# Feed-forward weights and the last rows of wo in long rows per partition; the result stored from columns, without a transpose

## The chip, the cores and the metric

The kernel runs on one core of one Trainium2 chip. The core has five instruction streams: TensorE (PE, matmuls and their weight loads), VectorE (DVE), ScalarE (ACT), GpSimd (POOL) and SyncE (SP), which here only issues DMA transfers. The transfers run on 16 DMA engines that share the queue of SP. The metric is the device time of one launch in microseconds: 689.65 us before the change, the median of 3 runs (689.49 to 689.85).

## The reference

One token (a row of 640 features) goes through an attention block over a cache of 16384 keys and values for each of 32 heads, and then through a gated feed-forward block. Each block is preceded by a layer norm with shift and scale that come from a conditioning vector, and followed by a gate and a residual.

```python
mod = (_silu(c) @ w_mod).reshape(c.shape[0], 6, 1, -1)
sa, ca, ga, sb, cb, gb = (mod[:, i] ...)
h = _layernorm(x) * (1 + ca) + sa
q = (h @ wq)                       # 32 heads of 128
scores = q . k_cache * 128 ** -0.5 # 32 x 16384
o = softmax(scores) . v_cache      # 32 x 128
x = x + ga * (o @ wo)              # wo: 4096 x 640
h = _layernorm(x) * (1 + cb) + sb
x = x + gb * ((_silu(h @ w_gate) * (h @ w_up)) @ w_down)   # 640 x 1728, 1728 x 640
```

K and V are 4 MB each per head in bfloat16, 268 MB in all; all weights together are some 22 MB.

## The kernel before

**Columns.** A vector of 640 features is kept as a tile of 128 partitions by 5 columns (`KC` = 5). A product of a vector with a matrix is made on TensorE with the matrix as the stationary operand: for each piece of 128 output features and each piece of 128 input features there is one weight load of 128 x 128 and one matmul with a single moving column. So the result again stands in columns. Which features stand in which partition follows from how the matrix was loaded and which of its columns a matmul takes. For the first half of the program feature 5p+k stands in partition p, column k: `c_col`, `x_col`, `w_mod` and `wq` are loaded with `(p k)`, five neighbouring rows per partition, and `mod_mm_a` (line 321) takes every fifth column of `w_mod`, beginning at k. From `mod_mm_b` on (line 355: the gate, shift and scale vectors that are used after attention) the kernel changes to feature 128k+p: there, and in wo and w_down, a matmul takes 128 adjacent columns, and gate and up are loaded with `(k p)`, so that each partition receives five separate rows of 3456 bytes.

**Heads.** For each head, DVE multiplies K with the broadcast q, folds the product three times and reduces it to scores (lines 420 to 435). GpSimd takes maximum and sum over partitions, ACT the exponentials. PE then multiplies probabilities and V with V as the moving operand, 32 matmuls of 512 columns (line 459). For the last head V is loaded in three parts and is the stationary operand instead (line 483), so that its last part needs only 32 small matmuls.

**From heads to wo.** The heads 0 to 27 form the groups of `GROUPS`: three of 8 and one of 4. Wo's rows for a group of n heads are loaded so that a partition gets n neighbouring rows. The attention output of a head stands in order in the partitions, so it has to be rearranged to match: `on` scales it, `z` (line 496, ACT) spreads it over a mask into `Z`, one matmul `am` (line 500, PE) with a small selection matrix sums it into place, and `as` (line 502, ACT) copies the group to `A_sb`. The heads 28 to 31 (`HD` = 28) skip this: their part of wo is loaded one row of 1280 bytes per partition and head (`dma_wo_rows`), and `on` (line 505) writes them to `On`, from which wo's matmuls (line 541) take them directly.

**Feed-forward.** The rows of gate's output 256j+2p+i stand in partition p (`NP2` pairs), so that a partition gets pairs of rows of w_down, 2560 bytes; gate and up (line 605) therefore take every second column. A thirteenth piece of 128 features and a rest of 64 come in rows of 1280 bytes. W_down is loaded in five transfers and multiplied in five groups (line 623), each waiting for its own.

**Residual and result.** As the second half has feature 128k+p, x is loaded a second time as five rows (`x_row`), transposed on PE and copied to `x_res` in the middle of the loop over heads (line 550). At the end the 128 x 5 result `o_col` is transposed on PE (line 631), copied by ACT (line 632) and stored as five rows of 256 bytes.

**Order.** Each operation is given an engine, a position and the operations that it depends on; `_Plan.emit` sorts each engine's operations by position and puts a semaphore wait ahead of one whose dependency isn't yet known to be done. An engine works strictly in that order. The positions are written by hand: `TK(h)` is the start of head h, `TL` that of the last head, `TE` = `TL` + 32 the end part. SP issues K of the next head when the slot is free, then V; wo is issued in the next to last head (`TO`), gate, up and w_down behind the last scores (`TW`), as they lie in the slots of K.

Of the kernel before, what the change touches and what calls it, by code (L numbers as in the profile page):

```python
# [6 lines left out]
BF16 = mybir.dt.bfloat16  # L7
F32 = mybir.dt.float32
ALU = mybir.AluOpType
ACTF = mybir.ActivationFunctionType  # L10
# [26 lines left out]
class _Plan:  # L37
# [21 lines left out]
    def op(self, eng, pos, fn, deps=(), name=""):  # L59
        o = _Op(eng, pos, fn, list(deps), name, len(self.ops))  # L60
        self.ops.append(o)
        return o
# [79 lines left out]
def build(nc, A_x, A_k, A_v, A_wq, A_wo, B_wg, B_wu, B_wd, c_in, w_mod, out):  # L142
    H, S, Dh = A_k.shape[1], A_k.shape[2], A_k.shape[3]
    D = A_x.shape[2]
# [7 lines left out]
    NP2 = NF // 2  # L152
    GQ = 4

    GROUPS = [(0, 8), (8, 8), (16, 8), (24, 4)]
    HD = 28
    assert H % GQ == 0 and all(128 % n == 0 for _, n in GROUPS) and GROUPS[-1][0] + GROUPS[-1][1] == HD < H
# [5 lines left out]
    def TK(h):  # L163
        return 20.0 + PERIOD * h

    es = ExitStack()
    with es:
# [3 lines left out]
        def sb(name, shape, dtype):  # L171
            return es.enter_context(nc.sbuf_tensor(name, list(shape), dtype))
# [31 lines left out]
        A_sb = sb("A_sb", [128, HD], BF16)  # L204
        On = sb("On", [128, H - HD], BF16)
        x_row = sb("x_row", [KC, 128], BF16)
        o_row = sb("o_row", [KC, 128], BF16)
        x_res = sb("x_res", [128, KC], F32)
# [146 lines left out]
        o_mod_b = op(PE, 4.5, lambda e: f_mod(e, wm_v, 2, 6, lambda o, k: slice(o + 128 * k, o + 128 * (k + 1))), deps=[d_wm, o_h], name="mod_mm_b")  # L355
# [50 lines left out]
        for h in range(H):  # L406
# [82 lines left out]
            if h < HD:  # L489
                g = [i for i, (h0, n) in enumerate(GROUPS) if h0 <= h < h0 + n][0]  # L490
                h0, n = GROUPS[g]
                jw = 128 // n
                o_on[h] = op(ACT, base + 29.0, lambda e, h=h, sc=sc: e.activation(  # L493
                    out=on_f[:, h:h + 1], in_=OT_ps[:, h:h + 1], func=ACTF.Copy, scale=sc),
                    deps=[done, o_rl], name="on%d" % h)
                o_z[h] = op(ACT, base + 29.2, lambda e, h=h, g=g, n=n, o=(h - h0) * jw, jw=jw: e.activation(  # L496
                    out=Z[:, g, o:o + jw], in_=msk[n][:], func=ACTF.Copy, scale=on_f[:, h:h + 1]),
                    deps=[o_on[h], o_msk[n]], name="z%d" % h)
                if h == h0 + n - 1:
                    o_am = op(PE, base + 29.4, lambda e, g=g, n=n: e.matmul(A_ps[:, 0:n], lhsT=Z[:, g], rhs=e8[n][:], start=True, stop=True),  # L500
                              deps=[o_z[i] for i in range(h0, h0 + n)] + [o_e8[n], o_as[g - 1] if g else None], name="am%d" % g)
                    o_as[g] = op(ACT, base + 29.6, lambda e, h0=h0, n=n: e.activation(out=A_sb[:, h0:h0 + n], in_=A_ps[:, 0:n], func=ACTF.Copy),
                                 deps=[o_am], name="as%d" % g)
            else:
                o_on[h] = op(ACT, base + 29.0 + (0.7 if h == H - 1 else 0.0), lambda e, h=h, sc=sc: e.activation(
                    out=On[:, h - HD:h - HD + 1], in_=OT_ps[:, h:h + 1], func=ACTF.Copy, scale=sc),
                    deps=[done, o_rl], name="on%d" % h)
# [5 lines left out]
        while a < len(GROUPS):  # L513
            b = a
            while b < len(GROUPS) and GROUPS[b][1] == GROUPS[a][1]:
# [7 lines left out]
        d_wo1 = plan.dma(TO + 0.1, wo_v[:, HD:H, :], A_wo[HD * 128:H * 128, :].rearrange("(k p) n -> p k n", p=128),  # L523
                         "wo1", deps=[o_mod_b, o_mod], name="dma_wo_rows")
        wo_seq = [(k, g) for g, (h0, n) in enumerate(GROUPS) for k in range(h0, h0 + n)] + [(k, None) for k in range(HD, H)]
        o_wo = []
        for g in list(range(len(GROUPS))) + [None] * (H - HD):
            if g is not None:
                ks = [k for k, gg in wo_seq if gg == g]
                deps, pos = [o_as[g], d_wo[g]], TL + 29.45 + 0.005 * g  # L530
            else:
                k = HD + len(o_wo) - len(GROUPS)
                ks = [k]
                deps, pos = [o_on[k], d_wo1], TL + (29.48 + 0.001 * (k - HD) if k < H - 1 else 29.8)

            def f_wo(e, ks=ks):
                last = None
                for k in ks:
                    rhs = A_sb[:, k:k + 1] if k < HD else On[:, k - HD:k - HD + 1]
                    for cc in range(KC):  # L540
                        last = e.matmul(attn_ps[:, cc:cc + 1], lhsT=wo_v[:, k, 128 * cc:128 * (cc + 1)], rhs=rhs,
                                        start=(k == 0 and cc == 0), stop=(k == H - 1 and cc == KC - 1), skip_group_check=True)
                return last
            o_wo.append(op(PE, pos, f_wo, deps=deps, name="wo%d" % len(o_wo)))


        HX = H // 2
        d_xr = plan.dma(TK(HX) + 8.95, x_row[:], A_x[0, 0].rearrange("(k p) -> k p", p=128), "xr", name="dma_x_row")
        xT_bf = st_ps[:, 256:256 + KC].bitcast(BF16)
        o_xT = op(PE, TK(HX) + 29.9, lambda e: e.transpose(xT_bf[:, 0:KC], x_row[:], ident[0:KC, 0:KC]), deps=[d_xr, o_ident, o_rstd], name="x_tr")  # L550
        o_xf = op(ACT, TK(HX) + 29.95, lambda e: e.activation(out=x_res[:], in_=xT_bf[:, 0:KC], func=ACTF.Copy), deps=[o_xT], name="x_res")

# [3 lines left out]
        d_wg = plan.dma(TW, wg_v, B_wg.rearrange("(k p) n -> p k n", p=128), "wg", deps=wdeps, name="dma_wg")  # L556
        d_wu = plan.dma(TW + 0.01, wu_v, B_wu.rearrange("(k p) n -> p k n", p=128), "wu", deps=wdeps, name="dma_wu")
        wd_parts = []
        d_wd = []

        def load_wd(a, b):
            i = len(d_wd)
            if b <= 2 * NP2:
                dst = wd_v[:, a:b, :].rearrange("p (j i) n -> p j (i n)", i=2)
                src = B_wd[128 * a:128 * b, :].rearrange("(j p i) n -> p j (i n)", p=128, i=2)
            elif b <= NF:
                dst, src = wd_v[:, a, :], B_wd[128 * a:128 * b, :]
            else:
                dst, src = wd_v[0:FR, a, :], B_wd[128 * a:F, :]
            d_wd.append(plan.dma(TW + 0.02 + 0.01 * i, dst, src, ("wd", i), deps=wdeps, name="dma_wd%d" % i))  # L570
            wd_parts.append((a, b))
        for a, b in ((0, 6), (6, 2 * NP2 - 2), (2 * NP2 - 2, 2 * NP2)):
            load_wd(a, b)
        for a in range(2 * NP2, FCH):
            load_wd(a, a + 1)
# [7 lines left out]
            out=x1[:], in0=tt2[:], scalar=1.0, in1=x_res[:], op0=ALU.mult, op1=ALU.add, accum_out=st[:, 4:5]),  # L583
# [12 lines left out]
        def f_gu(e, wv, ps_t):  # L596
            last = None
            for j in range(FCH):
                for k in range(KC):
                    if j < 2 * NP2:  # L600
                        cols = slice(256 * (j // 2) + j % 2, 256 * (j // 2 + 1), 2)
                    else:
                        cols = slice(128 * j, min(128 * (j + 1), F))
                    w = 128 if j < NF else FR
                    last = e.matmul(ps_t[0:w, j:j + 1], lhsT=wv[:, k, cols], rhs=h2_col[:, k:k + 1],
                                    start=(k == 0), stop=(k == KC - 1))
            return last
# [9 lines left out]
        for i, (a, b) in enumerate(wd_parts):  # L617
            def f_down(e, a=a, b=b):
                last = None
                for cc in range(KC):  # L620
                    for k in range(a, b):
                        kw = 128 if k < NF else FR
                        last = e.matmul(f_ps[:, cc:cc + 1], lhsT=wd_v[0:kw, k, 128 * cc:128 * (cc + 1)], rhs=gu_col[0:kw, k:k + 1],  # L623
                                        start=(k == 0 and cc == 0), stop=(k == FCH - 1 and cc == KC - 1), skip_group_check=True)
                return last
            prev = op(PE, TE + 1.8 + 0.01 * i, f_down, deps=[o_gum, d_wd[i], prev], name="down%d" % i)
# [3 lines left out]
        oT_bf = A_ps[0:KC, 256:320].bitcast(BF16)  # L630
        o_tr = op(PE, TE + 2.1, lambda e: e.transpose(oT_bf, o_col[:], ident[:]), deps=[o_oc, o_ident], name="o_tr")  # L631
        o_or = op(ACT, TE + 2.2, lambda e: e.activation(out=o_row[:], in_=oT_bf, func=ACTF.Copy), deps=[o_tr], name="o_row")
        d_out = plan.dma(TE + 2.3, out[0, 0].rearrange("(c p) -> c p", p=128), o_row[:], "out", deps=[o_or], name="dma_out")
# [49 lines left out]
```

## Time and profile before

| | us |
|---|---|
| time, median of 3 runs | 689.65 |
| span of the profiled execution, first to last instruction | 684.5 |
| DVE busy | 617.5 |
| PE busy | 351.0 |
| POOL busy | 360.0 |
| ACT busy | 79.6 |
| HBM read | 290.48 MB, 424 GB/s over the span |

The profiled execution is told by its span alone; no device time of its own is listed beside it. The time of the runs lies 5.15 us above that span: this is what lies around the first and last instruction, and it is carried over when a span is turned into a time.

Three stretches follow each other. Up to about 31 us w_mod and wq arrive and q is made. Up to 651.5 us the heads run, one each 19 to 20 us. From there on no more scores are computed: the last V, gate, up and w_down arrive, and PE works on what has arrived. The DMA queue of SP is busy for 99.1% of the span. PEclk is the granted TensorE clock; in the last 30 us it is 0.50 for the most part.

In lines of the timeline the first number is the start and the second the duration from the first start to the last end, both in us; then come engine, line, operation, output and input, shapes and count, and in brackets the engine's idle time before the group and what ended it. A line at the chain of waits has the start, the length and what the end was waiting for.

### The profile page before, as it was taken

To read this page: it belongs to the slowest core of one execution; us is meant where nothing else is said; L and a number is where in the kernel's file an instruction comes from. 1 tells how busy PE (TensorE), PEld (TensorE's weight loads), DVE (VectorE), ACT (ScalarE), POOL (GpSimd) and SP (SyncE) were. 2 spreads that over 40 slices of the span, in tenths; PEclk is the share of its full clock that TensorE was granted. 3 is DMA by queue.
4 is the path that set the end of the run, shared out by engine and by line. 5 is a ranking of instruction groups with operands and counts; after the bars stand their busy time and mean duration, and the time that the engine had idled before them with its cause. 6 is when DMAs were issued, how large, how long until landed. Compare 5 with 4: busy or idle time off the path is not lost.

```text
span 684.5 us, 4723 instructions
## 1 busy us (share of the span) xinstructions
PE 351.0 (51%) x1941; PEld 150.8 (22%) x1942; DVE 617.5 (90%) x226; ACT 79.6 (12%) x281; POOL 360.0 (53%) x71
## 2 busy tenths in 40 slices
PE   0545344656554454655554444565544545655464
PEld 0322111222221121222221121222211212222154
DVE  0299999999999999999999999999999999999911
ACT  0111011011101111011101111011101110111010
POOL 0005765655567765655567766655533644555400
PEclk9976677676677667677777767767776677677765
DMA  8999999999999999999999999999999999999997
GB/s 369 417 438 432 431 429 437 429 433 433 429 434 431 431 429 430 433 431 434 433 431 429 433 429 431 430 431 433 432 433 433 429 432 429 435 433 428 413 413 277
DMA packets 13979, 290.79 MB, mean 425 GB/s; under 512 B 1605, under 2 KB 2309, under 8 KB 4485
## 3 DMA queue, kind: packets, MB, share of 16 engines
q1 hardware_dynamic: 13668, 290.48, 99.1%
q8 instruction: 15, 0.25, 0.1%
q10 hardware_dynamic: 288, 0.00, 0.0%
q14 instruction: 8, 0.06, 0.0%
HBM read 290.48 MB, written 0.00 MB: 424 GB/s over the span
## 4 chain that ended last, share of the span: by engine, by line
DVE 79%; DMA 18%; SPq 2%; issue 1%; PE 0%; ACT 0%; DVEq 0%
DVE kring L420 35%; DVE kring L422 18%; DVE kring L429 14%; DMA kring<-in_A_k_cache_dram 12%; DVE S_sb L432 9%; DMA vbig<-in_A_wq_dram 4%; SPq L71 2%; DMA kring<-in_B_w_down_dram 2%; DVE pm L435 1%; PE psb L339 0%; PE psb L623 0%; ACT qbc L343 0%; DVE e L402 0%; DVE msk L397 0%; PE psb L631 0%
## 5 line engine op out<-in xcount | busy, mean ns | idle before, releaser
L459 PE MATMUL psb<-vbig,P_sb 128*4 128x512 bf16 x992 | 284.4, 458 | 268.1 <-ACT P_sb L442 193.9
L438 POOL PARTITION_ALL_REDUCE gm<-pm x32 | 229.2, 7163 | 239.9 <-DVE pm L435 239.9
L420 DVE TENSOR_TENSOR kring<-kring,qbc 128x16384 bf16<-128x16384 bf16 (+1 forms) x35 | 278.4, 7953 | 5.9 <-ACT qbc L343 4.6
L459 PEld LDWEIGHTS psb<-vbig,P_sb 128*4 128x4 bf16 x992 | 94.8, 98 | 444.6 <-ACT P_sb L442 219.9
L445 POOL PARTITION_ALL_REDUCE Ls<-rs x32 | 129.7, 4054 | 34.2 <-ACT P_sb L442 34.2
L422 DVE TENSOR_TENSOR kring<-kring 128x8192 bf16<-128x8192 bf16 (+1 forms) x35 | 142.1, 4059 | 1.2
L429 DVE TENSOR_TENSOR kring<-kring 128x4096 bf16<-128x4096 bf16 x64 | 112.5, 1758 | 2.2
L432 DVE TENSOR_REDUCE S_sb<-kring 128x128 f32<-128x2048 bf16 x32 | 73.2, 2286 | 1.1
L472 PE MATMUL psb<-ident_f,acc_sb 4*128 4x1 f32 x248 | 32.5, 248 | 23.8 <-ACT acc_sb L465 23.8
L465 ACT ACTIVATE acc_sb<-psb,rl 4x512 f32<-4x512 f32 x31 | 21.0, 677 | 176.2 <-PE psb L459 176.2
L472 PEld LDWEIGHTS psb<-ident_f,acc_sb 4*128 4x128 f32 x248 | 29.8, 186 | 39.5 <-ACT acc_sb L465 39.5
L440 ACT ACTIVATE nb<-gm 128x1 f32<-128x1 f32 x32 | 6.4, 201 | 193.6 <-POOL gm L438 193.6
L447 ACT ACTIVATE lnl<-Ls 128x1 f32<-128x1 f32 x32 | 6.5, 203 | 133.7 <-POOL Ls L445 133.7
L580 DVE TENSOR_TENSOR tt<-attn_bf,modb 128x5 f32<-128x5 bf16 x1 | 0.2, 166 | 14.5 <-ACT attn_bf L579 14.5
L442 ACT ACTIVATE P_sb<-S_sb,nb 128x128 bf16<-128x128 f32 x32 | 12.9, 402 | 1.2
L289 PE MATMUL psb<-st,ones_f 128*128 128x1 f32 x4 | 1.2, 363 | 22.8 <-ACT x_f L306 22.1
L339 PE MATMUL psb<-vbig,h_col 128*128 128x512 bf16 x39 | 10.8, 448 | 2.4 <-DMA vbig<-in_A_wq_dram 2.4
L291 DVE SCALAR_TENSOR_TENSOR xc<-x_f,psb 128x5 f32<-128x5 f32 x1 | 0.2, 161 | 12.2 <-PE psb L289 12.2
L435 DVE TENSOR_REDUCE pm<-S_sb 128x1 f32<-128x128 f32 x32 | 9.2, 286 | 1.1
L496 ACT ACTIVATE Z<-msk,on_f 128x16 bf16<-128x16 f32 (+1 forms) x28 | 8.7, 310 | 0.9
L493 ACT ACTIVATE on_f<-psb 128x1 f32<-128x1 f32 x28 | 4.8, 171 | 31.9 <-PE psb L472 30.7
L283 DVE TENSOR_SCALAR dd<-ec 128x5 f32<-128x5 f32 x1 | 0.2, 172 | 8.9 <-ACT ec L282 8.9
(72 smaller groups left out, 78.3 us busy)
## 6 DMA issues: line engine op xcount, KB each, us to landing
kring<-in_A_k_cache_dram SPq DMA_DIRECT2D x31, 4096.0 KB, 18.4
vbig<-in_A_v_cache_dram SPq DMA_DIRECT2D x31, 4096.0 KB, 27.6
vbig<-in_A_wq_dram SPq DMA_DIRECT2D x1, 5120.0 KB, 26.5
wreg<-in_w_mod_dram SPq DMA_DIRECT2D x1, 4800.0 KB, 14.6
kring<-in_A_k_cache_dram SPq DMA_DIRECT2D x4, 1024.0 KB, 31.4
wreg<-in_A_wo_dram SPq DMA_DIRECT2D x1, 3840.0 KB, 38.0
kring<-in_B_w_gate_dram SPq DMA_DIRECT2D x1, 2160.0 KB, 18.9
kring<-in_B_w_up_dram SPq DMA_DIRECT2D x1, 2160.0 KB, 23.8
```

Source lines behind the costliest of these rows:

```text
L71: return e.dma_start(out_ap, in_ap)
L420: o_m = op(DVE, base + 3.3 * c, lambda e, ksl=ksl, qb=qb: e.tensor_tensor(out=ksl, in0=ksl, in1=qb, op=ALU.mult), deps=[d_k[h][c], o_qbc[h ...
L422: fd.append(op(DVE, base + 3.3 * c + 2.2 + (6.6 if npc == 1 else 0.0), lambda e, ksl=ksl: e.tensor_tensor(out=ksl[:, :, 0:64], in0=ksl[:, ...
L429: prev = [op(DVE, base + 15.5 + 1.5 * i, lambda e, kslot=kslot, w=w: e.tensor_tensor(out=kslot[:, :, 0:w], in0=kslot[:, :, 0:w], in1=kslot ...
L432: o_red[h] = op(DVE, base + 18.2, lambda e, s2=s2, kslot=kslot, w=w: e.tensor_reduce(out=S_sb[:, s2], in_=kslot[:, :, 0:w], axis=AX.X, op= ...
L435: o_max = op(DVE, base + 18.5, lambda e, h=h, s2=s2: e.tensor_reduce(out=pm[:, h:h + 1], in_=S_sb[:, s2], axis=AX.X, op=ALU.max), deps=[o_ ...
L438: o_gm = op(POOL, base + 19.0, lambda e, h=h: e.partition_all_reduce(gm[:, h:h + 1], pm[:, h:h + 1], channels=128, reduce_op=bass.bass_isa ...
L442: o_exp[h] = op(ACT, base + 19.4, lambda e, h=h, s2=s2: e.activation(out=P_sb[:, s2], in_=S_sb[:, s2], func=ACTF.Exp, scale=SCALE, bias=nb ...
L445: o_L = op(POOL, base + 20.0, lambda e, h=h: e.partition_all_reduce(Ls[:, h:h + 1], rs[:, h:h + 1], channels=128, reduce_op=bass.bass_isa. ...
L459: last = e.matmul(acc_ps[s2][0:4, :], lhsT=P_sb[:, s2, 4 * c:4 * c + 4], rhs=vring[:, s2, 4 * c:4 * c + 4, :].rearrange("p t d -> p (t d)" ...
L465: o_acc[h] = op(ACT, base + 28.6, lambda e, h=h, s2=s2: e.activation(out=acc_sb[:, s2], in_=acc_ps[s2][0:4, :], func=ACTF.Copy, scale=rl[0 ...
L472: last = e.matmul(OT_ps[:, h:h + 1], lhsT=acc_sb[:, s2, 128 * i:128 * (i + 1)], rhs=ident_f[:, i:i + 1], start=(i == 0), stop=(i == 3))
```

## The change

- Gate and up are loaded with `(p k)`: five neighbouring rows, 17280 bytes, per partition. Their inputs therefore stand as feature 5p+k.
- W_down's first 13 x 128 rows are loaded with `(p k)`: 13 neighbouring rows per partition, in three transfers of 6, 5 and 2 rows. The rest of 64 rows is now the first transfer. Gate and up take every 13th column, beginning at j, to match (inner feature 13p+j).
- Wo's matmuls, w_down's matmuls and `mod_mm_b` take every fifth column, beginning at k, so that all vectors of 640 features stand as 5p+k.
- Heads 28 to 31 form a fifth group of 4 and go through `z`, `am` and `as` like the others. Their part of wo comes in rows of 5120 bytes, in one transfer with that of heads 24 to 27. Wo's last group is one of four heads (20 matmuls) behind `as4`; before, head 31's five matmuls alone were left.
- x is no longer loaded a second time; the residual takes `x_f32`. The transpose of the result and its copy go, and `o_col` is stored directly: 128 pieces of 10 bytes.

```diff
-    GROUPS = [(0, 8), (8, 8), (16, 8), (24, 4)]
-    HD = 28
+    GROUPS = [(0, 8), (8, 8), (16, 8), (24, 4), (28, 4)]
...
-        o_mod_b = op(PE, 4.5, lambda e: f_mod(e, wm_v, 2, 6, lambda o, k: slice(o + 128 * k, o + 128 * (k + 1))), deps=[d_wm, o_h], name="mod_mm_b")
+        o_mod_b = op(PE, 4.5, lambda e: f_mod(e, wm_v, 2, 6, lambda o, k: slice(o + k, o + D, KC)), deps=[d_wm, o_h], name="mod_mm_b")
...
-            if h < HD:
-                g = [i for i, (h0, n) in enumerate(GROUPS) if h0 <= h < h0 + n][0]
...
-            else:
-                o_on[h] = op(ACT, base + 29.0 + (0.7 if h == H - 1 else 0.0), lambda e, h=h, sc=sc: e.activation(
-                    out=On[:, h - HD:h - HD + 1], in_=OT_ps[:, h:h + 1], func=ACTF.Copy, scale=sc),
-                    deps=[done, o_rl], name="on%d" % h)
+            g = [i for i, (h0, n) in enumerate(GROUPS) if h0 <= h < h0 + n][0]
+            h0, n = GROUPS[g]
+            jw = 128 // n
+            late = 0.6 if h == H - 1 else 0.0
+            o_on[h] = op(ACT, base + 29.0 + late, lambda e, h=h, sc=sc: e.activation(
+                out=on_f[:, h:h + 1], in_=OT_ps[:, h:h + 1], func=ACTF.Copy, scale=sc),
+                deps=[done, o_rl], name="on%d" % h)
+            o_z[h] = op(ACT, base + 29.2 + late, lambda e, h=h, g=g, n=n, o=(h - h0) * jw, jw=jw: e.activation(
+                out=Z[:, g, o:o + jw], in_=msk[n][:], func=ACTF.Copy, scale=on_f[:, h:h + 1]),
+                deps=[o_on[h], o_msk[n]], name="z%d" % h)
...
-        d_wo1 = plan.dma(TO + 0.1, wo_v[:, HD:H, :], A_wo[HD * 128:H * 128, :].rearrange("(k p) n -> p k n", p=128),
-                         "wo1", deps=[o_mod_b, o_mod], name="dma_wo_rows")
...
-                        last = e.matmul(attn_ps[:, cc:cc + 1], lhsT=wo_v[:, k, 128 * cc:128 * (cc + 1)], rhs=rhs,
+                        last = e.matmul(attn_ps[:, cc:cc + 1], lhsT=wo_v[:, k, cc:D:KC], rhs=A_sb[:, k:k + 1],
...
-        d_xr = plan.dma(TK(HX) + 8.95, x_row[:], A_x[0, 0].rearrange("(k p) -> k p", p=128), "xr", name="dma_x_row")
-        xT_bf = st_ps[:, 256:256 + KC].bitcast(BF16)
-        o_xT = op(PE, TK(HX) + 29.9, lambda e: e.transpose(xT_bf[:, 0:KC], x_row[:], ident[0:KC, 0:KC]), deps=[d_xr, o_ident, o_rstd], name="x_tr")
-        o_xf = op(ACT, TK(HX) + 29.95, lambda e: e.activation(out=x_res[:], in_=xT_bf[:, 0:KC], func=ACTF.Copy), deps=[o_xT], name="x_res")
...
-        d_wg = plan.dma(TW, wg_v, B_wg.rearrange("(k p) n -> p k n", p=128), "wg", deps=wdeps, name="dma_wg")
-        d_wu = plan.dma(TW + 0.01, wu_v, B_wu.rearrange("(k p) n -> p k n", p=128), "wu", deps=wdeps, name="dma_wu")
+        d_wg = plan.dma(TW, wg_v, B_wg.rearrange("(p k) n -> p k n", p=128), "wg", deps=wdeps, name="dma_wg")
+        d_wu = plan.dma(TW + 0.01, wu_v, B_wu.rearrange("(p k) n -> p k n", p=128), "wu", deps=wdeps, name="dma_wu")
+        wd_src = B_wd[0:128 * NF, :].rearrange("(p k) n -> p k n", p=128)
+        wd_parts = [(NF, FCH)] + [(0, NF // 2), (NF // 2, NF - 2), (NF - 2, NF)]
...
-                    if j < 2 * NP2:
-                        cols = slice(256 * (j // 2) + j % 2, 256 * (j // 2 + 1), 2)
-                    else:
-                        cols = slice(128 * j, min(128 * (j + 1), F))
+                    cols = slice(j, 128 * NF, NF) if j < NF else slice(128 * NF, F)
...
-                        last = e.matmul(f_ps[:, cc:cc + 1], lhsT=wd_v[0:kw, k, 128 * cc:128 * (cc + 1)], rhs=gu_col[0:kw, k:k + 1],
-                                        start=(k == 0 and cc == 0), stop=(k == FCH - 1 and cc == KC - 1), skip_group_check=True)
+                        last = e.matmul(f_ps[:, cc:cc + 1], lhsT=wd_v[0:kw, k, cc:D:KC], rhs=gu_col[0:kw, k:k + 1],
+                                        start=(i == 0 and cc == 0), stop=(i == len(wd_parts) - 1 and cc == KC - 1), skip_group_check=True)
...
-        oT_bf = A_ps[0:KC, 256:320].bitcast(BF16)
-        o_tr = op(PE, TE + 2.1, lambda e: e.transpose(oT_bf, o_col[:], ident[:]), deps=[o_oc, o_ident], name="o_tr")
-        o_or = op(ACT, TE + 2.2, lambda e: e.activation(out=o_row[:], in_=oT_bf, func=ACTF.Copy), deps=[o_tr], name="o_row")
-        d_out = plan.dma(TE + 2.3, out[0, 0].rearrange("(c p) -> c p", p=128), o_row[:], "out", deps=[o_or], name="dma_out")
+        d_out = plan.dma(TE + 2.3, out[0, 0].rearrange("(p k) -> p k", p=128), o_col[:], "out", deps=[o_oc], name="dma_out")
```

## The prediction

> **What bounds the kernel now.** I read the page's forty slices first, then the chain that ended last, then the timeline of the tail, and last the start, where one matrix product already reads weights with a stride. In the slices the transfers are busy from end to end.
>
> ```profile
> PEclk9976677676677667677777767767776677677765
> DMA  8999999999999999999999999999999999999997
> GB/s 369 417 438 432 431 429 437 429 433 433 429 434 431 431 429 430 433 431 434 433 431 429 433 429 431 430 431 433 432 433 433 429 432 429 435 433 428 413 413 277
> ```
>
> Up to 651.5 us it is the loop over heads (DVE 90% busy, 430 GB/s), which the change leaves alone. From there the chain is the DMA queue up to the last rows of w_down, then ten matmuls, two groups of five, two DVE steps, a transpose, a copy and the store:
>
> ```profile
> 666.96 13.59 DMA kring<-in_B_w_down_dram
> 680.55 0.09 issue
> 680.64 0.42 PE psb L623 x10
> ...
> 681.61 0.28 PE psb L623 x5
> ...
> 682.12 0.18 DVE o_col L629
> ...
> 682.34 0.28 PE psb L631
> ...
> 682.64 0.27 ACT o_row L632
> ```
>
> TensorE in the tail: gate and up run 70 matmuls each in 2.2 us and wait for data before each (up waits 3 us). So there is slack in gate, little in up, none in the last 2 us.
>
> ```profile
> 667.54 0.59 PE L289 MATMUL psb<-st,ones_f 128*128 128x1 f32 x2 [0.67 <-DVE x L582]
> 670.55 2.22 PE L605 MATMUL psb<-h_col,kring 128*128 128x1 bf16 x70 [1.25 <-DMA kring<-in_B_w_gate_dram]
> 675.74 2.25 PE L605 MATMUL psb<-h_col,kring 128*128 128x1 bf16 x70 [2.97 <-DMA kring<-in_B_w_up_dram]
> 682.94 0.31 SPq L71 DMA_DIRECT2D out_dram<-o_row  x1
> ```
>
> The start shows what a stride costs. The first 50 matmuls of L317 read columns 5 elements apart, the later 100 adjacent ones:
>
> ```profile
> 22.10 0.59 PE L289 MATMUL psb<-st,ones_f 128*128 128x1 f32 x2 [22.10 <-ACT x_f L306]
> 23.72 2.12 PE L317 MATMUL psb<-silu_c,wreg 128*128 128x1 bf16 x50
> 28.22 0.15 PEld L339 LDWEIGHTS psb<-vbig,h_col 128*128 128x128 bf16 x1 [0.28 <-issue]
> 28.65 0.15 PEld L339 LDWEIGHTS psb<-vbig,h_col 128*128 128x128 bf16 x1 [0.28 <-issue]
> 38.90 2.64 PE L317 MATMUL psb<-silu_c,wreg 128*128 128x1 bf16 x100
> ```
>
> Less one matmul's length (0.16 to 0.18 us) that is 40 ns from start to start at stride 5, against 25 ns. Gate, at stride 2, is 27 ns; its last five, 64 columns wide, take 54. Is the 40 from the clock? The rows of L289 last 0.59 us at 22.1 and again at 667.5, where the granted clock is 0.50, and the 512-wide products step by 0.43 us at 28 us and 0.21 after 32.9. So the first 50 ran at the tail's half clock: 40 against 27 is the stride.
>
> **The change part by part.** The sum is against the profiled span of 684.5 us; the median of 689.65 lies 5.15 above it, and I carry that over.
>
> *Loads.* 7.29 MB (gate, up and w_down 2160 KB each, 640 KB of wo) go in longer rows. The trace's packet records give medians of 56 ns for 1280 B, 102 for 2560, 135 for 3456, 199 for 5120, 389 for 10240, 1218 for 32768: about 9 ns plus 0.037 ns per byte. Wo's rows: 512 x 56 become 128 x 199, over 16 engines 0.2 us less. Gate and up: 640 x 135 become 128 x 647, 0.2 each. W_down: 768 x 102 and 128 x 56 become 128 each of 7680, 6400 and 2560 B, 0.2. Together 0.8; the slices agree (413 GB/s in the tail, 433 before it: 17.65 against 16.85 us). Ends: 0, if the tail's rate is not due to row length, and 1.0. So V of the last head lands 0.2 earlier, up 0.4 to 0.5 earlier (issued 651.95, landing 23.8 later, so 675.3), the last part of w_down at about 680.4 instead of 681.2.
>
> *Issues on SP.* Three DMAs go: x_row in the loop, one of wo's three (groups 24 and 28 share one), one of w_down's five. They took 0.4 us each or waited with a full queue ahead; nothing starves, gain nil. Wo of heads 24 to 27 then waits for that joint load (about 654.5) and starts near 657: hidden by the 112 matmuls ahead of it.
>
> *x_row, its transpose and copy*, and *stride 5 in mod_mm_b* (100 x 40 instead of 25 ns, end 43.1 instead of 41.6): next readers are DVE at 51.8 and PE at 57.5. Hidden by the first head; uncovered it would be 1.5. *Wo of the first 28 heads*: 140 matmuls at 40 ns are 5.6 instead of 3.85 us, 653.5 to 659.1, before V of the last head arrives at 660. Hidden by 0.8 us. *z28 to z30*, 0.31 us each on ACT, 12% busy, are hidden under the DVE loop.
>
> *The last group.* Heads 28 to 31 now go through Z, a matmul and A_sb, and head 31's part of it follows the last V. The same steps of head 27:
>
> ```profile
> 595.57 0.32 ACT L496 ACTIVATE Z<-msk,on_f 128x32 bf16<-128x32 f32 x1
> ...
> 595.95 0.18 PE L500 MATMUL psb<-e,Z 128*128 128x4 bf16 x1 [0.62 <-ACT Z L496]
> 596.16 0.17 ACT L502 ACTIVATE A_sb<-psb 128x4 bf16<-128x4 f32 x1 [0.27 <-PE psb L500]
> ```
>
> From the end of the row before (595.54) to A_sb at 596.33 are 0.8 us; then 20 matmuls at 40 ns instead of 5 at 27, 0.7 more. On PE the wait for z31 holds up wo, the second layer norm and gate, which need it anyway; on ACT attn_bf waits behind as4. H2, ready at 670.29, comes at 671.55 (+0.8 +0.7 -0.2), and gate starts at 671.6 instead of 670.55. Its data is there.
>
> *Gate and up at stride 13.* No row has this stride. Ends: 27 ns (stride 2 costs nothing) and 107 (twice the 54 ns of the 64-wide loads, a column at a time). Nearest is stride 5. A flat price for any long stride would be its 40 ns again; a price in proportion to the distance would be 40 x 13/5 = 104, the upper end. One row cannot tell the two apart, so I take the geometric middle, **64 ns**, and keep both for the range. Then gate lasts 2.25 + 64 x 0.037 = 4.6 us, to 676.2, past up's landing, and up runs on to 680.8. So the wait for up's data becomes PE time: what is late next is PE itself.
>
> The skill speaks on this. The Trainium skill, "SBUF — State Buffer", section "Door 1: The DMA port swizzle", says that SBUF is read in lines of 16 bytes, that each change of line costs, and that bf16 can be strided by up to 8 elements for free. The row at stride 5 (40 against 27 ns) contradicts the free 8. By the rule wo and down would cost 27 ns a matmul and the sum would be 1.1 us lower, 691.1; by the row it is the one below. From its lines alone one gets an estimate near mine: 32 columns at stride 5 cross 20 lines in 40 ns, at stride 13 they touch 32.
>
> *Down.* gu follows up by 0.3 us (677.99 to 678.33 in before), so 681.1. All of w_down has landed. Four groups, 70 matmuls at 40 ns, with 0.3 us between groups (before's last two groups start 0.42 apart for 0.11 of matmuls): 2.65 + 0.95 + 0.2 = 3.8, to 684.9, against 681.89.
>
> *Store.* Before, from the last matmul to the store's issue 1.05 us; without transpose and copy 0.45, so 685.35 against 682.94: +2.4. The store has 128 pieces of 10 B instead of 5 of 256. A like form, c_col's load, issues in 0.40 against 0.31 us. Ends: 0 and +1.5 (an output of its own kind, never timed; before's whole way from issue to span end is 1.6); I take 0.2, nearest to the issue row.
>
> Sum: +2.6 us, span 687.1, time **692.2**.
>
> **Rivals.**
> (1) *Not slower: stride 13 costs no more than stride 5.* For it: one penalty for any stride past a few bytes fits the one row as well. Against: 40 ns is less than two reads of 27. Then gate ends at 674.7, up waits for 675.3 and ends at 678.4, down at 682.5; less 0.6, plus 0.2: 689.85. With no stride price anywhere (against the row) the last landing decides and it is 689.2. Each ns at stride 13 is 0.128 us, so it decides at 54 ns: above that it is slower by over 0.2% (1.4 us, what a measurement of this kernel can tell).
> (2) *A column at a time, 107 ns.* For it: the 64-wide loads. Against: stride 5 is 40, not 107. Gate and up take 7.4 each: 697.8. At 80 ns, three cycles of the half clock per column, 694.3.
> (3) *The store is slow.* 10-byte writes to memory, 1.5 us later to land: 693.5 with the rest as forecast. Nothing in this trace speaks for or against. The Trainium skill, "DMA: Bandwidth & Descriptors", section "Specifications", puts the line-rate limit at 512 B and says that smaller writes read first; 256 and 10 B are both below it.
> (4) *The loads are no faster.* Only 0.2 of the 0.8 is in my sum, since down starts after the last landing: 692.4, the same case in effect.
>
> **How the numbers follow.** Forecast, 50 to 85 ns at stride 13, 0.58 (with rival 4), its own range 690.5 to 695; rival 1 0.25; rival 2 at 107 ns 0.10; rival 3 0.07. The range runs from rival 1 with a store as quick as now, 689.3, to 80 ns with a store 0.7 later, 695.0. Faster, 0.05: rival 1 with more gain in the loads than the rows give. Same, 0.25: the rest of rival 1 and the forecast's low edge. Slower, 0.70.
>
> **What would show it.** Gate and up some 4.6 us each with no wait for data between; down in four groups of 40 ns a matmul; last group's z, matmul and copy 0.8 us; loads done near 680.4, well before PE; no DMA at the end of the chain but the store. It is wrong if up still waits for its data, if stride 5 in the tail is 27 ns, or if the store lands over 2 us after its issue.

## The result, and the profile after

After the change the kernel takes 692.47 us (median of 4 runs, 692.19 to 693.89) against 689.68 before (4 runs, 689.49 to 689.85): 2.8 us slower, a ratio of 1.0046 with a 95% interval of 1.0033 to 1.0059. The forecast was 692.2, slower, with a range of 689.3 to 695.0.

The forty slices of the page, after: the transfers are as busy as before, but the last slice falls from 277 to 177 GB/s.

```profile
DMA  9999999999999999999999999999999999999994
GB/s 382 404 436 400 416 427 427 429 431 433 427 432 433 429 435 426 437 429 432 431 433 427 433 435 429 432 431 431 432 433 427 431 432 435 433 425 430 420 426 177
```

The chain that ended last, after (start, length, what the end waited for). Behind up's weights it now holds no transfer: TensorE, three steps of DVE (one of them, `tt`, is left out below), and then the store.

```profile
654.40 0.30 DVE pm L429
...
654.76 23.78 DMA kring<-in_B_w_up_dram
678.54 0.05 issue
678.59 4.42 PE psb L562 x70
...
683.10 0.18 DVE gu_col L571
...
683.83 1.35 PE psb L580 x30
...
685.32 1.15 PE psb L580 x25
...
686.60 0.55 PE psb L580 x10
...
687.37 0.17 DVE o_col L586
```

The timeline of the tail, after. Gate (673.98) and up (678.59) take 4.4 us each, where they took 2.2; up's wait for data has shrunk from 3.0 to 0.2 us. Wo of the first 28 heads takes 5.76 us instead of 3.85.

```profile
656.88 5.76 PE L519 MATMUL psb<-A_sb,wreg 128*128 128x1 bf16 x140
669.54 0.96 PE L519 MATMUL psb<-A_sb,wreg 128*128 128x1 bf16 x20 [0.27 <-ACT A_sb L496]
673.98 4.42 PE L562 MATMUL psb<-h_col,kring 128*128 128x1 bf16 x70 [1.05 <-DVE h_col L549]
678.59 4.40 PE L562 MATMUL psb<-h_col,kring 128*128 128x1 bf16 x70 [0.19 <-DMA kring<-in_B_w_up_dram]
687.56 0.35 SPq L71 DMA_DIRECT2D out_dram<-o_col  x1
```

The span of the page after is 690.5 us, 6.0 more than that of before, while the runs differ by 2.8. The two profiled executions did not begin alike. ACT's first two groups, before and then after:

```profile
9.70 0.21 ACT L282 ACTIVATE ec<-c_col 128x5 f32<-128x5 bf16 x1 [6.73 <-DMA c_col<-in_c_dram]
21.75 0.21 ACT L306 ACTIVATE x_f<-x_col 128x5 f32<-128x5 bf16 x1 [11.84 <-DMA x_col<-in_A_x_dram]
```

```profile
15.52 0.21 ACT L276 ACTIVATE ec<-c_col 128x5 f32<-128x5 bf16 x1 [12.53 <-DMA c_col<-in_c_dram]
28.02 0.21 ACT L300 ACTIVATE x_f<-x_col 128x5 f32<-128x5 bf16 x1 [12.29 <-DMA x_col<-in_A_x_dram]
```

In the second, x arrives 6.3 us later, and with it q and the first scores: the first head's maximum starts at 50.75 us before and at 55.57 after. To compare the ends, I count from the start of the last maximum of scores (L435 before, L429 after; "the last scores" below), when gate's load is issued: 651.53 and 654.40 us. From there to the end of the span it is 33.0 us before and 36.1 after: **3.1 us**. The rest of the 6.0 lies ahead of that point, where nothing that the change does explains it.

### The profile page after: what moved, and what is told of

Same layout as the page of the kernel before. It is cut to its first block, busy times and chain, and to the rows that moved or that the text cites. A ratio compares the mean times of both kernels' runs of the same rounds, so it can differ in the third digit from the quotient of the medians.

```text
span 690.5 us, 4719 instructions
## 1 busy us (share of the span) xinstructions
PE 361.5 (52%) x1940; PEld 159.6 (23%) x1941; DVE 616.9 (89%) x226; ACT 81.1 (12%) x284; POOL 381.3 (55%) x71
## 4 chain that ended last, share of the span: by engine, by line
DVE 89%; DMA 7%; PE 2%; issue 1%; ACT 0%; ACTq 0%; DVEq 0%; SPq 0%
DVE kring L414 40%; DVE kring L416 21%; DVE kring L423 16%; DVE S_sb L426 11%; DMA x_col<-in_A_x_dram 4%; DMA kring<-in_B_w_up_dram 3%; DVE pm L429 1%; PE psb L562 1%; PE psb L580 0%; PE psb L311 0%; PE psb L333 0%; ACT qbc L337 0%; PE psb L283 0%; PE psb L290 0%; DVE e L396 0%
## 5 line engine op out<-in xcount | busy, mean ns | idle before, releaser
L432 POOL PARTITION_ALL_REDUCE gm<-pm x32 | 262.3, 8198 | 226.7 <-DVE pm L429 226.7
L439 POOL PARTITION_ALL_REDUCE Ls<-rs x32 | 117.9, 3683 | 29.7 <-ACT P_sb L436 29.7
L466 PE MATMUL psb<-ident_f,acc_sb 4*128 4x1 f32 x248 | 32.5, 248 | 23.8 <-ACT acc_sb L459 23.8
L466 PEld LDWEIGHTS psb<-ident_f,acc_sb 4*128 4x128 f32 x248 | 29.8, 186 | 39.5 <-ACT acc_sb L459 39.5
L436 ACT ACTIVATE P_sb<-S_sb,nb 128x128 bf16<-128x128 f32 x32 | 12.9, 402 | 1.2
L429 DVE TENSOR_REDUCE pm<-S_sb 128x1 f32<-128x128 f32 x32 | 9.2, 286 | 1.1
L562 PE MATMUL psb<-h_col,kring 128*128 128x1 bf16 (+1 forms) x140 | 8.8, 199 | 1.2 <-DVE h_col L549 1.0
```

The source lines that it names most:

```text
L429: o_max = op(DVE, base + 18.5, lambda e, h=h, s2=s2: e.tensor_reduce(out=pm[:, h:h + 1], in_=S_sb[:, s2], axis=AX.X, op=ALU.max), deps=[o_ ...
L432: o_gm = op(POOL, base + 19.0, lambda e, h=h: e.partition_all_reduce(gm[:, h:h + 1], pm[:, h:h + 1], channels=128, reduce_op=bass.bass_isa ...
L436: o_exp[h] = op(ACT, base + 19.4, lambda e, h=h, s2=s2: e.activation(out=P_sb[:, s2], in_=S_sb[:, s2], func=ACTF.Exp, scale=SCALE, bias=nb ...
L439: o_L = op(POOL, base + 20.0, lambda e, h=h: e.partition_all_reduce(Ls[:, h:h + 1], rs[:, h:h + 1], channels=128, reduce_op=bass.bass_isa. ...
L466: last = e.matmul(OT_ps[:, h:h + 1], lhsT=acc_sb[:, s2, 128 * i:128 * (i + 1)], rhs=ident_f[:, i:i + 1], start=(i == 0), stop=(i == 3))
```

## The experiments

My theory: the end part costs 3.1 us, of which reading at stride 13 is the largest share, the store second, and the rows of the loads next to nothing. The rivals: the transfers are the bound and the stride is hidden; or the 6 us are all the change's. The first four kernels shared one chip, with before at 689.72 us (33 runs, 688.82 to 691.04). Each is one part undone, or one part done alone.

**Pairs again (`e1_pairs`).** After, with inner features in pairs of rows, so that gate and up read at stride 2:

```diff
-        wd_parts = [(NF, FCH)] + [(0, NF // 2), (NF // 2, NF - 2), (NF - 2, NF)]
+        wd_parts = [(NF, FCH), (NF - 1, NF), (0, 6), (6, 10), (10, 12)]
...
-                    cols = slice(j, 128 * NF, NF) if j < NF else slice(128 * NF, F)
+                    if j < 12:
+                        cols = slice(256 * (j // 2) + j % 2, 256 * (j // 2 + 1), 2)
+                    else:
+                        cols = slice(128 * j, min(128 * (j + 1), F))
```

> The kernel after, with the inner features as pairs of rows again: gate and up take every second column instead of every 13th, w_down comes in rows of 2560 and 1280 bytes in five transfers; everything else as after. Theory A (TensorE reading at stride 13 is the bound of the end): gate and up take 2.25 us each instead of 4.4, up waits for its data again, down keeps 40 ns a matmul with one more group, and the time falls by about 1.8 us, to 690.7. Theory B (the transfers are the bound and the stride is hidden): no change, 692.4, or slower by 0.2 through the shorter rows.

Measured: 691.55 us, 1.0021 of before (1.0012 to 1.0029). Its timeline:

```profile
655.77 0.33 SPq L71 DMA_DIRECT2D kring<-in_B_w_gate_dram  x1
675.33 2.25 PE L570 MATMUL psb<-h_col,kring 128*128 128x1 bf16 x70 [1.04 <-DVE h_col L554]
679.28 2.09 PE L570 MATMUL psb<-h_col,kring 128*128 128x1 bf16 x67 [1.71 <-DMA kring<-in_B_w_up_dram]
687.00 0.36 SPq L71 DMA_DIRECT2D out_dram<-o_col  x1
```

Gate is 2.25 us again, up waits for its data again, and the store is issued 31.2 us behind the last scores instead of 33.2: 1.9 us less, as theory A has it. Against the 692.47 us of the first measurement, in other rounds, the time fell by only 0.9. In the profiled execution the loop over heads took 1.4 us longer than in that of after: the last head took 20.8 us, where after's took 19.4. It varies in the other profiles too, from 19.3 us (`e2_store`) to 20.3 (after, profiled a second time) and 21.1 (`e7_ladder`). So the spans differ by up to 1.8 us that lie ahead of the end part. What makes that head longer, and whether it was longer in the other runs of this kernel, is not known.

**Adjacent columns (`e6_adjacent`)**, the same question with the loads of after left as they are:

```diff
-                    cols = slice(j, 128 * NF, NF) if j < NF else slice(128 * NF, F)
+                    cols = slice(128 * j, min(128 * (j + 1), F))
```

> The kernel after with gate and up taking 128 adjacent columns instead of every 13th; loads, down, wo and the store as after. Gate's outputs then don't match w_down's rows, so the result isn't the reference's. Theory A (the stride of 13 is most of the loss): gate and up 2.2 us each, up waits for its data until 24.1 us behind the last scores, the store is issued at 31.2 instead of 33.2; 2.0 faster than after, 690.5. Theory B (stride hidden): 692.5.

Measured: 691.22 us, on another chip, where after took 693.94 in the same rounds (below): 2.7 us less.

```profile
654.82 0.33 SPq L71 DMA_DIRECT2D kring<-in_B_w_gate_dram  x1
674.79 2.25 PE L562 MATMUL psb<-h_col,kring 128*128 128x1 bf16 x70 [1.04 <-DVE h_col L549]
678.88 2.09 PE L562 MATMUL psb<-h_col,kring 128*128 128x1 bf16 x67 [1.84 <-DMA kring<-in_B_w_up_dram]
686.14 0.35 SPq L71 DMA_DIRECT2D out_dram<-o_col  x1
```

The store is issued 31.3 us behind the last scores, as expected. With it theory B is out: the stride of 13 is on the path and worth 1.8 to 1.9 us there. The other parts of the change are all in this kernel. Its end part is 34.2 us against 33.0 before, and its store is issued when before's was (31.3 and 31.4): what they add lies behind that issue. The stride of 5 in wo and w_down has no run of its own.

**A ladder of strides (`e7_ladder`).** Gate and up of after, their 13 full chunks read at 13 different column steps:

```diff
+        STRIDES = [1, 2, 3, 4, 5, 6, 7, 8, 10, 12, 13, 16, 26]
...
+                    s = STRIDES[j] if j < NF else 1
+                    b0 = o0 + 1000 * k
+                    last = e.matmul(ps_t[0:w, j:j + 1], lhsT=kflat[:, b0:b0 + (w - 1) * s + 1:s], rhs=h2_col[:, k:k + 1],
```

> The kernel after with the 13 full chunks of gate and of up reading at column steps of 1, 2, 3, 4, 5, 6, 7, 8, 10, 12, 13, 16 and 26 elements, five matmuls each, instead of 13 throughout; the result isn't the reference's. Step of the starts within a chunk, at the half clock. Theory A (a price per memory line of 16 bytes: the more columns share a line the cheaper): 27 ns up to step 4, rising from 5 (40) to 8, and flat at about 60 from 8 on. Theory B (in proportion to the distance): 40 at 5, 64 at 8, 80 at 10, 104 at 13, 208 at 26. Theory C (a step of more than 8 bytes costs one flat addition): 40 from 5 on; excluded for 13 by the profile after, kept for the shape between 5 and 10.

The median step from start to start within a chunk, from the trace's start times, at a granted clock of 0.50 (gate and up agree within 2 ns):

| step, elements | 1, 2 | 3 | 4 | 5 | 6 | 7 | 8 | 10, 12, 13 | 16 | 26 |
|---|---|---|---|---|---|---|---|---|---|---|
| ns a matmul | 27 | 28 | 32 | 39 | 47 | 54 | 61 | 61 | 62 | 66 |

Theory A holds nearly to the number. 128 columns of 2 bytes lie on 16 lines of 16 bytes at step 1, on 32 at step 2 and so on, and on 128 lines from step 8 on; 61 ns over 128 lines is 0.48 ns a line, which gives 38, 46 and 53 at steps 5, 6 and 7. Below some 60 lines the 27 ns cover it. In proportion to distance (104 at 13) and a flat addition (40 from 5 on) are both out; the small rise at 26 is not explained. The Trainium skill, "SBUF — State Buffer", section "Door 1: The DMA port swizzle", names lines of 16 bytes, and the ladder agrees; it calls a stride of 8 bf16 elements free, where the ladder has 61 ns instead of 27.

**The store alone (`e2_store`).** Before, with `o_col` stored as it stands:

```diff
-        oT_bf = A_ps[0:KC, 256:320].bitcast(BF16)
-        o_tr = op(PE, TE + 2.1, lambda e: e.transpose(oT_bf, o_col[:], ident[:]), deps=[o_oc, o_ident], name="o_tr")
-        o_or = op(ACT, TE + 2.2, lambda e: e.activation(out=o_row[:], in_=oT_bf, func=ACTF.Copy), deps=[o_tr], name="o_row")
-        d_out = plan.dma(TE + 2.3, out[0, 0].rearrange("(c p) -> c p", p=128), o_row[:], "out", deps=[o_or], name="dma_out")
+        d_out = plan.dma(TE + 2.3, out[0, 0].rearrange("(p k) -> p k", p=128), o_col[:], "out", deps=[o_oc], name="dma_out")
```

> The kernel before with the result stored straight from the 128 x 5 columns, without transpose and copy (its 640 numbers land in another order than the reference's). Theory A (the small pieces land late): issue 0.6 us earlier, landing 2.6 us behind the issue instead of 1.2, together +0.8: 690.5. Theory B (the forecast's price, 0.2): 0.4 us faster than before, 689.3.

Measured: 690.36 us, 0.6 more than before (ratio 1.0008, interval 1.0000 to 1.0017, just at the edge of what can be told from zero). The trace is clearer. Its store starts at 685.25 us and the span ends at 688.1, 2.9 us later; in before it was 1.6. Of its store the trace says, issue to landing:

```profile
685.25 0.35 SPq L71 DMA_DIRECT2D out_dram<-o_col  x1
...
DMA to landing us min/median/max: 2.5/2.5/2.5
```

So the shortcut loses: without transpose and copy 0.6 us are won, and 1.3 to 1.4 lost by 128 pieces of 10 bytes instead of 5 of 256. The loss lies behind the packets: in after the last 10-byte packet ends 1.0 us behind the issue (688.60 us) and the landing follows 1.5 us later; in before the last packet of 256 bytes ends 0.9 us behind the issue (683.79), and the landing follows after 0.3. Whether the number of the pieces or their size makes it was not tried.

**The fifth group alone (`e3_group`).** Before, with `GROUPS` and the steps `z`, `am`, `as` of after for heads 28 to 31, and adjacent columns in wo:

```diff
-    GROUPS = [(0, 8), (8, 8), (16, 8), (24, 4)]
-    HD = 28
+    GROUPS = [(0, 8), (8, 8), (16, 8), (24, 4), (28, 4)]
+    HD = 32
...
```

> The kernel before with heads 28 to 31 as a fifth group through Z, a matmul and A_sb, wo's rows for them 5120 bytes, all columns as before. Theory A (hidden behind up's data): the second norm's output comes some 1.0 us later, up still waits for its weights, time as before, 689.7 within 0.3. Theory B (the chain from the last V sets the end): +1.0 us, 690.7.

Measured: 689.59 us, 0.9993 of before (0.9981 to 1.0005). The timeline shows the cover:

```profile
655.40 0.38 SPq L71 DMA_DIRECT2D kring<-in_B_w_gate_dram  x1
674.68 2.24 PE L589 MATMUL psb<-h_col,kring 128*128 128x1 bf16 x70 [1.04 <-DVE h_col L573]
679.70 2.25 PE L589 MATMUL psb<-h_col,kring 128*128 128x1 bf16 x70 [2.78 <-DMA kring<-in_B_w_up_dram]
686.82 0.31 SPq L71 DMA_DIRECT2D out_dram<-o_row  x1
```

Gate starts 0.3 us later than before, up still waits 2.8 us, and the store is issued 31.4 us behind the last scores, as before. Alone, the longer chain costs nothing. In after the cover is gone, and gate's start counts.

**The loads alone (`e4_loads`).**

```diff
-        d_wg = plan.dma(TW, wg_v, B_wg.rearrange("(k p) n -> p k n", p=128), "wg", deps=wdeps, name="dma_wg")
-        d_wu = plan.dma(TW + 0.01, wu_v, B_wu.rearrange("(k p) n -> p k n", p=128), "wu", deps=wdeps, name="dma_wu")
+        d_wg = plan.dma(TW, wg_v, B_wg.rearrange("(p k) n -> p k n", p=128), "wg", deps=wdeps, name="dma_wg")
+        d_wu = plan.dma(TW + 0.01, wu_v, B_wu.rearrange("(p k) n -> p k n", p=128), "wu", deps=wdeps, name="dma_wu")
...
+        wd_src = B_wd[0:128 * NF, :].rearrange("(p k) n -> p k n", p=128)
+        wd_parts = [(NF, FCH)] + [(0, NF // 2), (NF // 2, NF - 2), (NF - 2, NF)]
```

> The kernel before with the long rows alone: gate and up loaded 17280 bytes per partition, w_down as 13 rows per partition in the four transfers of after; matmuls keep their adjacent or every-second columns, so features and weights don't match and the result isn't the reference's. Theory A (row length is worth little at the end: in the profile after, up landed 24.1 us behind the last scores, before 24.2, and the last of w_down 29.4 instead of 29.6): 0 to 0.3 us faster, 689.5. Theory B (the packet prices of the forecast): up 0.5 and the last part 0.6 earlier, with one group of down less 0.3 more: 688.8.

Measured: 689.53 us, 0.9996 of before (0.9987 to 1.0005): nothing that this can tell from zero. In its trace the last piece of w_down lands 29.8 us behind the last scores, in before's 29.6. Gate's and up's packets are as cheap as forecast (644 ns for 17280 bytes; all of them over 16 engines 10.5 instead of 10.8 us), but w_down's of 7680 bytes took 308 ns (327 in after) and not 293. A gain of 0.3 is in the packet times; none has reached the landing.

**After once more, and the start.** The two spans of the pages differ by 6.0 us and the times by 2.8. Three pairs of kernels go after that.

> The kernel after, unchanged, timed beside before in the same rounds. Theory A (the profile of before caught an early start; the difference of the two is in the end part alone, 36.1 instead of 33.0 us behind the last scores): +2.5 to +3.1, 692.2 to 692.8, in nearly every run. Theory B (the 6.0 us between the two profiled spans are the change's): +6, 695.5.

Measured: 693.94 us (4 runs, 693.42 to 695.21), and before, in the same rounds on that chip, **686.08** (7 runs, 685.83 to 686.39). Neither theory had this. By these times, before started early on that chip every time, as in its profile, and after late every time; the 7.9 us between them are not like against like. After is also 1.5 us slower here than in the first measurement, and its profile, of the run of 695.21 us, has 37.0 us behind the last scores instead of 36.1: the last V landed 0.7 us later in it, the store was issued 0.4 later and took 0.5 longer to the end of the span. So the 2.8 and the 3.1 us hold for one set of rounds and one pair of profiles. On a third chip before itself did both: 3 of 21 runs lay between 685.94 and 686.50, the others between 688.97 and 691.35; of `e3_group` one run of 11 took 685.94. So before has two times, about 3.5 us apart, and 689.68 is the later one.

The edit of the next pair puts c and x on SP's queue, ahead of w_mod:

```diff
-        d_c = plan.dma(0.0, c_col[:], c_in[0].rearrange("(p k) -> p k", p=128), "c", name="dma_c", eng="act")
-        d_x = plan.dma(0.01, x_col[:], A_x[0, 0].rearrange("(p k) -> p k", p=128), "x", name="dma_x", eng="act")
+        d_c = plan.dma(-0.2, c_col[:], c_in[0].rearrange("(p k) -> p k", p=128), "c", name="dma_c")
+        d_x = plan.dma(-0.1, x_col[:], A_x[0, 0].rearrange("(p k) -> p k", p=128), "x", name="dma_x")
```

> The kernel before with the loads of c and x on SP's queue, ahead of w_mod, instead of on ACT's. Theory A (x, landing at 28 us in most executions and at 21.7 in the one profiled before, holds up q and with it the first scores): x lands in the first 5 us, q waits for wq alone, the first scores end near 50.7 us instead of 55.5; the loop then gives back up to 2 us to the transfers; 3 us faster than before, 686.5. Theory B (the loop is bound by the transfers, the start is given back): 689.7.

> The kernel after with the same edit, c and x ahead of w_mod on SP's queue. Theory A: as much faster than after as the other is than before, 689.5, and 2.8 to 3.1 behind the other. Theory B: 692.5.

Measured, on the chip of the early before: 686.89 and 690.49 us, 3.6 apart. x is there at 3.0 us in both, and the last scores begin at 652.72 us in both, so this pair differs in its end part alone: 32.5 and 36.0 us. After gained 3.5 us by the edit. `cx_before` is 0.8 us above an early before (1.0012, 0.9998 to 1.0026, which does not rule out zero); w_mod and all behind it is issued 0.9 us later in it.

The last pair leaves the queues alone and tests the mechanism. In the traces of the late starts, the 10-byte packets of c and x are spread out between 3.8 and 28.1 us, over the time of w_mod and wq. From 3.0 to 4.5 us, for instance, 16 of them start in after, as many as there are DMA engines, while a packet of w_mod (38400 bytes) takes 1.42 us: about one small packet per large one on each engine, eight of them for each vector. In the early one the first fifth of them is through by 2.4 us: there the first 10-byte packet starts at 1.80 us, ahead of the first of w_mod at 1.85; in after w_mod is first, at 1.82, and c follows at 3.90. So:

```diff
-        d_wm = plan.dma(0.0, wm_v, wm_src, "wm", name="dma_wmod")
+        d_wm0 = plan.dma(0.0, wm_v[:, 0:1, :], wm_src[:, 0:1, :], "wm0", name="dma_wmod0")
+        d_wm = plan.dma(0.02, wm_v[:, 1:KC, :], wm_src[:, 1:KC, :], "wm", name="dma_wmod")
...
```

> The kernel before with w_mod loaded in two transfers, first one row of 7680 bytes per partition, then the four others; c and x stay on ACT's queue. Theory A (each 10-byte packet of c and x gets its turn only after one packet of the large transfer on the same DMA engine, 8 each; with packets of 7680 bytes, 0.3 us, c's eight turns take 2.4 us instead of 12): c lands near 5 us, x near 14, both ahead of w_mod and wq, so q starts at 28 us and the time is 686.1 to 686.5, in every run: 3.4 faster where before takes 689.7, the same where before takes 686.1. Theory B (the late start has another cause): as before.

> The kernel after with the same two transfers of w_mod. Theory A: the late start is gone from it too, and what is left between it and the other is the end part: 36.0 against 32.5 to 33.0 us behind the last scores, 689.5, that is 3.0 to 3.5 slower than the other. Theory B: 692.5 to 694.

Measured: 686.00 us (10 runs, 685.84 to 686.28; 0.9953 of before, 0.9938 to 0.9967) and 689.52 us (12 runs, 689.13 to 689.80). By their times every run of both is an early one, and the two profiles show it; x in `split_before`:

```profile
15.89 0.21 ACT L307 ACTIVATE x_f<-x_col 128x5 f32<-128x5 bf16 x1 [9.66 <-DMA x_col<-in_A_x_dram]
```

A first transfer of short rows lets c through at 5.9 to 6.0 us and x at 15.7 to 15.9, ahead of wq, which lands near 28. From 3.0 to 4.5 us 78 of the 10-byte packets start in `split_before`, against 16 in after, with packets of 7680 bytes beside them that take 0.29 us. The turn-taking is thereby shown as the cause of the late start; why c is sometimes first in before, on one chip in all of 7 runs, and in none of the 8 runs of after, stays open. (The Trainium skill, "DMA: Bandwidth & Descriptors", section "Queues, rings and completion order", says that a DMA engine goes round its queues packet by packet; the records here, one small for one large, agree if each of them is such a packet.)

Two conclusions. `split_before` is 3.6 us faster than before, whose runs beside it mostly started late, and steadier; after's first measurement, in other rounds, lies 6.5 us above it. And with the start fixed the change costs **3.5 us**, a third more than the forecast's 2.6. Where both start late, it is the 2.8 of the first measurement; why that is less was not found.

The ends of the fixed pair, `split_before` and then `split_after`:

```profile
651.74 0.38 SPq L71 DMA_DIRECT2D kring<-in_B_w_gate_dram  x1
675.46 2.25 PE L606 MATMUL psb<-h_col,kring 128*128 128x1 bf16 x70 [2.85 <-DMA kring<-in_B_w_up_dram]
682.77 0.30 SPq L71 DMA_DIRECT2D out_dram<-o_row  x1
```

```profile
651.62 0.33 SPq L71 DMA_DIRECT2D kring<-in_B_w_gate_dram  x1
671.15 8.79 PE L563 MATMUL psb<-h_col,kring 128*128 128x1 bf16 x140 [1.05 <-DVE h_col L550]
684.51 0.35 SPq L71 DMA_DIRECT2D out_dram<-o_col  x1
```

From the last scores to the store it is 31.0 and 32.9 us; gate and up of `split_after` run through as one group of 140, with no wait between them.

## Why the prediction was right, and where not

The direction and the mechanism were right. That its sum of +2.6 came out so close to the 2.8 is in part luck: the store was issued 0.6 us earlier than forecast and took 1.2 longer to end, and the 5.15 us carried over were something else than it said. By its steps, before's and after's profiles counted from the last scores:

| step | forecast | measured |
|---|---|---|
| second norm's output later | +1.25 | +0.77 |
| gate, up, each | 4.6 | 4.4 |
| up's end later | +2.8 | +2.1 |
| down, first matmul to last | 3.8 | 3.8 |
| last matmul to store's issue | 0.45 | 0.43 |
| store's issue later | +2.4 | +1.8 |
| issue to the span's end later | +0.2 | +1.4 |
| sum | +2.6 | +3.1 |

- *Stride 13* was the forecast's largest unknown, taken as the middle of 40 and 104 ns. It is 60, where the forecast took 64; no step of the ladder reaches the 80 or 107 ns of rival 2. The mechanism held: up's wait for data became TensorE time (0.2 us of it are left in this profile, nothing in the second one of after and in `split_after`), and, the store aside, no transfer is left in the chain after up's weights. The reason given for the middle, that one row can't tell the ends apart, was fair; the ladder shows that there was a rule to find.
- *The store* was mis-sized: 0.2 was taken from the row of an issue, +1.4 was measured. The upper end of 1.5 was right, and so was rival 3's price; its chance of 0.07 was too small. What was counted was the time to issue 128 pieces, and not the time for them to land. The prediction also calls itself wrong if the store lands over 2 us after its issue: it landed after 2.6 us, so that sign came, while the other two did not (up waited 0.2 us instead of 3.0, and a stride of 5 takes 40 ns, not 27).
- *The last group*: from the last V's landing (13.6 and 12.9 us behind the last scores) to the second norm's output it is 1.5 us more, as forecast. It came out 0.5 earlier since V landed 0.7 earlier, not 0.2. Gate's and up's longer rows did not bring that (`e4_loads` has 13.8 us); `e3_group`, with those of wo alone, has 12.9, but the second profile of after 13.6 again, so the cause stays open.
- *The loads*: forecast 0.8 for all, and up 0.4 to 0.5 earlier. Up landed as before (24.1 against 24.2 us), the last of w_down 0.2 earlier. It cost the sum little, as no group of down waits for its data in after. But its sign "loads done near 680.4, well before PE" did not quite come: the last two rows of w_down landed at 683.85 us, 0.5 us behind down's first matmul (683.33) and 2.7 ahead of the group that reads them (686.60).
- *Hidden work*: wo's 5.8 us ran up to 662.6, just past the landing of V's first part at 662.3. So the cover of 0.8 us was used up and a little more. Nothing of it shows in the end, as PE then waited for V's last part (1.4 us).
- *What lies around the span*: the forecast carried 5.15 us over from the difference of a median and a span. In the runs with both numbers it is 1.7 to 1.9. The other 3.4 were the early start of the one profiled execution. That did no harm, as after starts late like the runs of before did, but the step was wrong, and that it did no harm was luck: had before's median been an early one (686.1), the forecast would have been some 4 us too low.
- *The range*: its lower end, rival 1 with a store as quick as now, is 689.65 by the prediction's own numbers (689.85 less the store's 0.2), not 689.3.

## What to carry to other kernels

A stationary operand read with a stride pays by the lines of 16 bytes that its columns touch: up to 3 bf16 elements free here, 39 ns at 5, 61 from 8 on. So longer rows for a load, which won nothing measurable here, are dearly bought if the engine behind it must then read with a stride, above all where that engine's slack is smaller than the price. Before a span and a median are set against each other, see whether they are executions of the same kind: a few lines at the start of the timeline tell. And two tiny loads on a second queue, which take turns with packets of 38 KB, can be the first thing to mend: one short transfer in front was worth 3.6 us where before starts late, as much as the whole change costs.

## What was not expected

- The result in 128 pieces of 10 bytes took 2.5 to 3.0 us from issue to landing. Five of 256 bytes were done, with the end of the program, 1.6 us behind their issue.
- The price of a stride of 5 does not follow TensorE's clock: `mod_mm_b` of after, at a granted clock of 1.00 (43.2 us), steps by 40 ns at stride 5, as w_down does at 0.50; with adjacent columns it was 25 (`mod_mm_b` of before) and 27.
- The same program takes 686.1 or 689.7 us by the turn that 10-byte packets get at the start: every run of before early on one chip, 3 of 21 on another, none of 33 on a third (its fastest was 688.82); the one run beside `e7_ladder`, on a fourth, was early too (686.02).
- Rows of 17280 bytes did not bring gate and up in earlier than rows of 3456: 24.0 to 24.5 us behind the last scores in the three kernels with long rows and a late start (`e6_adjacent` 24.0, after 24.1, `e4_loads` 24.5), 24.2 in before.
